# Reordering the seven quarter products of an output projection, and moving two early steps

## The chip, the cores and the metric

The kernel runs on one core of one Trainium2 chip. The metric is the device time of one execution in microseconds (us), as the median of several runs. The engines are TensorE (PE, with its weight loads shown apart as PEld), VectorE (DVE), ScalarE (ACT), GpSimd (POOL) and SyncE (SP), which starts most of the transfers.

## The reference, cut to what matters

Attention with a top-32 mask feeds a SwiGLU feed-forward network. Everything is float32.

```python
batch, n_heads, seq, head_dim = (8, 8, 576, 64)
n_tokens, d_model, d_ff = (4608, 512, 1536)

def _attn_ref(q, k, v):
    scores = scale * np.matmul(q, k.transpose(0, 1, 3, 2))
    kth = np.partition(scores, -top_k, axis=-1)[..., -top_k:-top_k + 1]   # top_k = 32
    scores = np.where(scores >= kth, scores, -1e9)
    scores = scores - np.max(scores, axis=-1, keepdims=True)
    attn = np.exp(scores)
    attn = attn / (np.sum(attn, axis=-1, keepdims=True) + 1e-09)
    return np.matmul(attn, v)

def _moe_ref(x, w_gate, w_val, w_out):      # x: attention output, (4608, 512)
    g = x @ w_gate
    silu = g * (1.0 / (1.0 + np.exp(-g)))
    return (silu * (x @ w_val)) @ w_out
```

## The kernel before: the parts that matter here

The attention works in 160 *units*: one batch, one tile of queries (128 rows, or the last 64), one pair of heads. Each unit passes through a pipeline that spans several turns: scores on TensorE, the top-32 search on VectorE (`select`), the mask added on GpSimd (`penalize`), the exponential on ScalarE (`weigh`), the scaling (`normalize`), a transposition on TensorE (`turn`) and the product with V (`values`). Beside it runs the feed-forward network in 18 *blocks* of 256 tokens. It is a Python generator (`feed`) that is advanced in *pieces* within each turn. A piece is either half of a product or half of a quarter product, and a credit decides how many pieces a turn holds.

Every engine executes its instructions in the order in which this program issues them. So the place at which a piece stands in a turn decides what an engine has to finish before it may go on.

One turn, cut to its order:

```python
        # turn n, head
        next(nxt, None)                  # odd n: scores of units n+1, n+2 (TensorE, ScalarE copies)
        next(nxt, None)
        if 0 <= n - 1 < NU:
            penalize(n - 1)              # GpSimd: bias (L391), e += sc (L393)
        flush(on_pool)                   # queued GpSimd work
        flush(on_act)                    # queued ScalarE work
        if n % 2 == 1 and n >= 5:
            finish_units([n - 5, n - 4]) # values
        early[0]()
        run(nxt)
        if 0 <= n - 1 < NU:
            weigh(n - 1)                 # ScalarE: exp (L402)
        dve(2, beside=False)
        # ...
        pieces(2)
        flush(on_act)
        if 0 <= n - TURN < NU:
            run(turn(n - TURN))          # transposes (L431), copies et (L432)
        dve(1)
        dve(1)
        next(norm, None)
        run(norm)                        # ScalarE: e *= 1/tot (L417)
        next(ahead, None)
        pieces(1)
        run(ahead)
        dve(1)
        pieces(1)
        dve(2)
        run(topk)                        # VectorE: rest of the top-32 search, mask (L381)
        pieces(6)
```

The second matrix product of a block (`silu * val @ w_out`) is done from the second block on with seven products of quarter size instead of eight, and with sums on GpSimd that prepare their operands and collect their results. `first` and `late` are the two halves of the 256 tokens. `T[1]` to `T[7]` are prepared combinations of `w_out`, `hs[0]` to `hs[5]` are the six tiles of the activation, and `s32` reuses the memory of the block's input `x`. Line numbers are those of the profile.

```python
        DH = DM // 2
        y_ps = ps_f.tile([P, 2, DH], FP32, tag="f", name="y_ps")   # tag "f": 3 buffers
        x_ps = ps_f.tile([P, 2, DH], FP32, tag="f", name="x_ps")
        def quarter(i, ps):
            for m in range(MQ):                        # MQ = 6
                s, r = m // 2, m % 2
                lhsT = {
                    1: lambda: hs[s][:, r, first],
                    2: lambda: hs[s + MS // 2][:, r, first],
                    3: lambda: hs[s][:, r, late],
                    4: lambda: hs[s + MS // 2][:, r, late],
                    5: lambda: hs[s][:, r, late],
                    6: lambda: s32[:, m],
                    7: lambda: s32[:, m],
                }[i]()
                nc.tensor.matmul(ps, lhsT, T[i][m], start=m == 0, stop=m == MQ - 1)  # L606
                if m % 3 == 2:
                    yield 0.75
        for s in range(MS // 2):                       # first sum, L613
            nc.gpsimd.tensor_tensor(s32[:, 2*s:2*s+2], hs[s][:, :, first], hs[s][:, :, late], ALU.subtract)
        yield from quarter(1, y_ps[:, 0])
        flush(on_act)
        flush(on_pool)
        for s in range(MS // 2):                       # second sum, L621
            nc.gpsimd.tensor_tensor(hs[s][:, :, late], hs[s][:, :, late], hs[s + MS // 2][:, :, late], ALU.add)
        yield from quarter(7, x_ps[:, 1])
        for s in range(MS // 2):                       # third sum, L626
            nc.gpsimd.tensor_tensor(s32[:, 2*s:2*s+2], hs[s][:, :, late], hs[s][:, :, first], ALU.subtract)
        yield from quarter(5, x_ps[:, 0])
        # keep_x: ScalarE copies x_ps to a (L633), GpSimd o = a0 + a1 (L592)
        on_act.append(keep_x)
        # keep_y: ScalarE copies y_ps to b (L640), GpSimd sum_up: three sums (L592)
        yield from quarter(6, y_ps[:, 1])
        on_act.append(keep_y)
        flush(on_act)
        flush(on_pool)
        for s in range(MS // 2):                       # fourth sum, L654
            nc.gpsimd.tensor_tensor(hs[s][:, :, late], hs[s + MS // 2][:, :, first], s32[:, 2*s:2*s+2], ALU.subtract)
        y_ps2 = ps_f.tile([P, DH], FP32, tag="f", name="y_ps")
        yield from quarter(2, y_ps2[:])
        # rest_y: ScalarE copies y_ps2 to o (L664), GpSimd o += b0 (L592)
        on_act.append(rest_y)
        x_ps2 = ps_f.tile([P, 2, DH], FP32, tag="f", name="x_ps")
        yield from quarter(4, x_ps2[:, 1])
        yield from quarter(3, x_ps2[:, 0])
        # rest_x: ScalarE copies x_ps2 (L676), GpSimd adds a (L592), stores
```

Before the first turn the loads and the first scores are issued. `rounding` and `early` advance the preparation of the weights: a transfer, two ScalarE steps (L121, L123), a GpSimd step (L126), VectorE and GpSimd steps (L130, L133), and a last VectorE step (L136). The VectorE steps are issued between those of the top-32 search.

```python
    load_all(0)
    rounding(2)
    load_all(1)
    run(fetch(0))          # transposes of the first pair's K and Q
    run(scores([0]))
    run(fetch(1))          # those of the second pair
```

Of the kernel before, what the change touches and what calls it, by code (L numbers as in the profile page):

```python
# [10 lines left out]
ALU = mybir.AluOpType  # L11
FP32 = mybir.dt.float32
# [4 lines left out]
P = 128  # L17
# [11 lines left out]
def kernel(  # L29
# [41 lines left out]
    nc = tc.nc  # L71
# [8 lines left out]
    MS = MC // 2  # L80
# [13 lines left out]
    ps_f = ctx.enter_context(tc.tile_pool(name="ps_f", bufs=3, space=PSUM))  # L94
# [117 lines left out]
    early = [lambda: None]  # L212
# [67 lines left out]
    def prep(i):  # L280

        parts = raw.pop(i)
        slab = slabs.tile([P, JP + S], FP32, tag="kqT", name="kqT")
        ahead = NHP <= i and i + 1 < len(pairs)
        for what, at in ((0, 0), (2, JP), (1, S)):
            ps = ps_t.tile([P, 512], FP32, tag="t", name="kqps")
            if what == 2:
                nc.tensor.transpose(
                    ps[:, 0:P], parts[2].rearrange("p h d -> p (h d)"), ident[:]
                )  # L290
                for d in HALVES:
                    nc.scalar.copy(klast[pairs[i][1]][d, d], ps[d, 0:R])
                nc.scalar.copy(slab[:, at : at + R], ps[:, R:P])
                if ahead:
                    load(i + 1, 2)
                yield
                continue
            for c in range(J):
                nc.tensor.transpose(
                    ps[:, c * P : (c + 1) * P],  # L300
                    parts[what][:, c].rearrange("p h d -> p (h d)"),
                    ident[:],
                )
            nc.scalar.copy(slab[:, at : at + JP], ps[:])

            if ahead and what == 0:
                load(i + 1, 1)
            elif ahead and i + 2 < len(pairs):
                load(i + 2, 0)
        preps[i] = slab  # L310
# [8 lines left out]
    def scores(ns):  # L319

        def bank(name):
            return ps_t.tile([P, 512], FP32, tag="t", name=name)

        qt = units[ns[0]][1]
        wide = R if qt == J else P
        at = JP if qt == J else S + qt * P
        queries = slice(at, at + wide)
        of = [(preps[units[n][0] * NHP + units[n][2]], units[n][2]) for n in ns]
        first = [bank("s")] if qt == J else [bank("s") for _ in HALVES]
        last = bank("last")  # L330
        for u, (slab, hp) in enumerate(of):
            if qt < J:
                nc.tensor.matmul(  # L333
                    last[:, u * P : (u + 1) * P], slab[:, queries], klast[hp][:]
                )
            else:
                for d in HALVES:
                    nc.tensor.matmul(
                        last[d, u * P : u * P + R], slab[d, queries], klast[hp][d, d]
                    )  # L340
        for u, (slab, hp) in enumerate(of):
            if u == 0:
                mains = first
            elif qt == J:
                mains = [bank("s")]
            else:
                mains = [bank("s") for _ in HALVES]
            for hh, d in enumerate(HALVES):
                ps = mains[0][d, :] if qt == J else mains[hh][:]
                nc.tensor.matmul(ps, slab[d, queries], slab[d, 0:JP])  # L350
            yield
            sc = work.tile([P, 2 * S], FP32, tag="sc", name="sc", bufs=3)
            state[ns[u]] = dict(sc=sc)
            nc.scalar.copy(sc[:, JP : JP + wide], last[:, u * P : u * P + wide])  # L354
            for hh, ps in enumerate(mains):
                nc.scalar.copy(sc[:, hh * (S + R) : hh * (S + R) + JP], ps[:])  # L356
# [137 lines left out]
    on_act, on_pool = [], []  # L494

    def flush(queue):
        while queue:
            queue.pop(0)()
# [7 lines left out]
    def feed(kb):  # L506
# [5 lines left out]
        hs = []  # L512

        def product(w, s, then):
# [17 lines left out]
        first, late = slice(0, P), slice(P, BLK)  # L532

        s32 = x[:].rearrange("p a b -> p (a b)")[:, 0 : MQ * P].rearrange(
            "p (m t) -> p m t", t=P
        )
# [20 lines left out]
        o = ffn.tile([P, 2, DM], FP32, tag="o", name="o", bufs=1)  # L557
# [27 lines left out]
        while len(T[3]) < MQ:  # L585
            next(weight)
        DH = DM // 2
        y_ps = ps_f.tile([P, 2, DH], FP32, tag="f", name="y_ps")
        x_ps = ps_f.tile([P, 2, DH], FP32, tag="f", name="x_ps")

        def tt(out, in0, in1):
            nc.gpsimd.tensor_tensor(out, in0, in1, ALU.add)  # L592

        def quarter(i, ps):
            for m in range(MQ):
# [10 lines that stand above are left out]
                nc.tensor.matmul(  # L606
                    ps, lhsT, T[i][m], start=m == 0, stop=m == MQ - 1
                )
                if m % 3 == 2:
                    yield 0.75  # L610

        for s in range(MS // 2):
            nc.gpsimd.tensor_tensor(  # L613
                s32[:, 2 * s : 2 * s + 2], hs[s][:, :, first], hs[s][:, :, late], ALU.subtract
            )
        yield from quarter(1, y_ps[:, 0])
        flush(on_act)
        flush(on_pool)

        for s in range(MS // 2):  # L620
            nc.gpsimd.tensor_tensor(  # L621
# [7 lines left out]
        yield from quarter(5, x_ps[:, 0])  # L629
        a = ffn.tile([P, 2, DH], FP32, tag="gv", name="p57", bufs=3)  # L630

        def keep_x():
            nc.scalar.copy(a[:], x_ps[:])  # L633
            on_pool.append(lambda: tt(o[:, 1, DH:], a[:, 0], a[:, 1]))

        on_act.append(keep_x)
        b = ffn.tile([P, 2, DH], FP32, tag="gv", name="p16", bufs=3)

        def keep_y():
            nc.scalar.copy(b[:], y_ps[:])  # L640

            def sum_up():
                tt(b[:, 1], b[:, 0], b[:, 1])
                tt(o[:, 1, DH:], o[:, 1, DH:], b[:, 1])
                tt(a[:], a[:], b[:, 1:2].to_broadcast([P, 2, DH]))

            on_pool.append(sum_up)

# [4 lines that stand above are left out]
        for s in range(MS // 2):  # L653
# [3 lines left out]
                s32[:, 2 * s : 2 * s + 2],  # L657
                ALU.subtract,
            )
        y_ps2 = ps_f.tile([P, DH], FP32, tag="f", name="y_ps")  # L660
        yield from quarter(2, y_ps2[:])

        def rest_y():
            nc.scalar.copy(o[:, 0, 0:DH], y_ps2[:])  # L664
            on_pool.append(lambda: tt(o[:, 0, 0:DH], o[:, 0, 0:DH], b[:, 0]))

        on_act.append(rest_y)
        x_ps2 = ps_f.tile([P, 2, DH], FP32, tag="f", name="x_ps")
        yield from quarter(4, x_ps2[:, 1])
        yield from quarter(3, x_ps2[:, 0])  # L670
# [20 lines left out]
    def piece():  # L691

        if len(on_act) > 1:
            flush(on_act)
        while True:
            if not current:
                if not todo or done.get(todo[0], 0) < NHP * BLK:
                    return 0
                flush(on_act)
                flush(on_pool)  # L700
                current.append(feed(todo.pop(0)))
            cost = next(current[0], 0)
            if cost == 0:
                current.pop()
                continue
            return cost

    def fetch(n):

        b, qt, hp = units[n]  # L710
        i = b * NHP + hp
        if qt == 0:
            yield from prep(i)
# [20 lines left out]
    def run(steps):  # L734
        for _ in steps:
            pass
# [10 lines left out]
    load_all(1)  # L747
    run(fetch(0))
    run(scores([0]))
    run(fetch(1))  # L750
    credit = [0.0]
    no = iter(())
# [119 lines left out]
```

## Time and profile before

| | before |
|---|---|
| time, median of 3 runs (lowest to highest) | 1862.27 us (1861.88 to 1864.19) |
| span of the profiled execution | 1858.6 us |
| PE busy | 1713.0 us, 92% |
| DVE busy | 1641.1 us, 88% |
| ACT busy | 1197.0 us, 64% |
| POOL busy | 1015.3 us, 55% |
| mean granted clock of TensorE | 0.955 of full speed |

Busy shares are means over the whole span. From about 20 to 200 us VectorE is busy nearly all the time and TensorE about half of it; from about 260 us TensorE is busy nearly all the time, and the last 100 us belong to TensorE with the last blocks. A line of the timeline gives start, length, engine, line, operation, tiles and count, and in brackets the idle time of the engine before it and what ended that.

### The profile page before, as it was taken

To read this page: it belongs to the slowest core of one execution; us is meant where nothing else is said; L and a number is where in the kernel's file an instruction comes from. 1 tells how busy PE (TensorE), PEld (TensorE's weight loads), DVE (VectorE), ACT (ScalarE), POOL (GpSimd) and SP (SyncE) were. 2 spreads that over 40 slices of the span, in tenths; PEclk is the share of its full clock that TensorE was granted. 3 is DMA by queue.
4 is the path that set the end of the run, shared out by engine and by line. 5 is a ranking of instruction groups with operands and counts; after the bars stand their busy time and mean duration, and the time that the engine had idled before them with its cause. 6 is when DMAs were issued, how large, how long until landed. Compare 5 with 4: busy or idle time off the path is not lost.

```text
span 1858.6 us, 29975 instructions
## 1 busy us (share of the span) xinstructions
PE 1713.0 (92%) x10500; PEld 1394.9 (75%) x10500; DVE 1641.1 (88%) x3409; ACT 1197.0 (64%) x2879; POOL 1015.3 (55%) x932
## 2 busy tenths in 40 slices
PE   4467889989999999999999999999999999999998
PEld 2236658768888878787888877878888878787886
DVE  6999999999999989998999979998999979999300
ACT  4656766667666676576767675766776667575431
POOL 3555747636565546555465636565457544656444
PEclk8558999989999999999999999999999999999999
DMA  6332220001200020001200021000300011000000
GB/s 174 91 91 85 63 63 27 1 12 30 57 4 12 1 64 26 12 1 27 50 25 1 13 52 38 1 12 7 71 14 12 1 45 26 12 1 12 1 12 12
DMA packets 104534, 58.56 MB, mean 32 GB/s; under 512 B 83904, under 2 KB 92096, under 8 KB 104384
## 3 DMA queue, kind: packets, MB, share of 16 engines
q1 hardware_dynamic: 103328, 56.39, 11.5%
q8 instruction: 83, 1.36, 0.3%
q14 instruction: 67, 0.55, 0.1%
q10 hardware_dynamic: 1056, 0.26, 0.1%
HBM read 47.19 MB, written 9.44 MB: 30 GB/s over the span
## 4 chain that ended last, share of the span: by engine, by line
PE 68%; ACT 10%; POOL 6%; DVE 2%; issue 1%; POOLq 0%; ACTq 0%
PE f L520 37%; PE av L459 7%; PE s L350 7%; PE x_ps L606 5%; PE etps L431 5%; PE y_ps L606 3%; ACT e L402 3%; POOL e L393 2%; ACT et L432 2%; PE av L466 2%; ACT e L417 2%; POOL p L592 1%; ACT sc L356 1%; PE last L333 1%; POOL h L654 1%; DVE m L371 1%
## 5 line engine op out<-in xcount | busy, mean ns | idle before, releaser
L371 DVE MAX8 m<-e 128x8 f32<-128x576 f32 x864 | 612.7, 744 | 2.2
L393 POOL TENSOR_TENSOR e<-e,sc 128x1152 f32<-128x1152 f32 (+1 forms) x160 | 382.8, 2392 | 336.8 <-DVE e L381 282.1
L375 DVE MATCH_REPLACE8 e<-m,e 128x576 f32<-128x576 f32 x576 | 423.0, 740 | 0.0
L520 PE MATMUL f<-xT,wv 128*128 128x256 f32 x1728 | 396.7, 380 | 0.0
L520 PE MATMUL f<-xT,wg 128*128 128x256 f32 x1728 | 395.5, 380 | 0.0
L520 PEld LDWEIGHTS f<-xT,wg 128*128 128x128 f32 x1728 | 323.9, 190 | 42.2 <-issue 0.5
L520 PEld LDWEIGHTS f<-xT,wv 128*128 128x128 f32 x1728 | 322.9, 190 | 41.1 <-ACT half_g L546 0.2
L402 ACT ACTIVATE e<-e,bias 128x576 f32<-128x576 f32 x288 | 224.5, 793 | 96.3 <-POOL e L393 96.3
L371 DVE MAX8 m<-sc 128x8 f32<-128x576 f32 x288 | 204.8, 746 | 63.8 <-ACT sc L356 45.2
L350 PE MATMUL s<-kqT 64*128 64x512 f32 (+1 forms) x640 | 197.5, 665 | 50.8 <-ACT et L432 41.1
L431 PE MATMUL etps<-ident,e 128*128 128x128 f32 x1312 | 178.9, 281 | 45.2 <-ACT e L417 21.8
L417 ACT ACTIVATE e<-e,tot 128x576 f32<-128x576 f32 x288 | 212.9, 794 | 5.6 <-DVE tot L414 5.6
L375 DVE MATCH_REPLACE8 e<-m,sc 128x576 f32<-128x576 f32 x288 | 211.4, 739 | 0.0
L431 PEld LDWEIGHTS etps<-ident,e 128*128 128x128 f32 x1312 | 157.4, 145 | 67.8 <-issue 32.8
L459 PEld LDWEIGHTS av<-et,v 128*64 128x64 f32 x2560 | 141.9, 147 | 79.2 <-ACT sc L356 66.8
L432 ACT COPY et<-etps 128x512 f32<-128x512 f32 (+1 forms) x448 | 182.3, 480 | 17.1 <-PE etps L431 17.1
L381 DVE TENSOR_SCALAR e<-sc,m 128x576 f32<-128x576 f32 x288 | 189.3, 693 | 1.1
L548 POOL TENSOR_TENSOR h<-h,half_g 128x512 f32<-128x512 f32 x108 | 139.3, 1290 | 91.4 <-ACT h L547 88.5
L356 ACT COPY sc<-s 128x512 f32<-128x512 f32 x288 | 159.5, 610 | 42.2 <-PE s L350 42.2
L553 POOL TENSOR_TENSOR h<-h,val 128x512 f32<-128x512 f32 x108 | 139.0, 1287 | 86.1 <-ACT val L552 83.1
L459 PE MATMUL av<-et,v 128*64 128x128 f32 (+1 forms) x2560 | 162.6, 282 | 12.1 <-ACT sc L356 11.3
L354 ACT COPY sc<-last 128x128 f32<-128x128 f32 (+1 forms) x160 | 42.5, 266 | 185.0 <-PE last L333 157.8
(75 smaller groups left out, 2043.4 us busy)
## 6 DMA issues: line engine op xcount, KB each, us to landing
v<-in_v_dram SPq DMA_DIRECT2D x32, 256.0 KB, 2.9
kq_in<-in_k_dram SPq DMA_DIRECT2D x63, 128.0 KB, 2.8
kq_in<-in_q_dram SPq DMA_DIRECT2D x63, 128.0 KB, 2.7
w<-in_moe_w_gate_dram SPq DMA_DIRECT2D x12, 512.0 KB, 3.8
w<-in_moe_w_val_dram SPq DMA_DIRECT2D x12, 512.0 KB, 3.7
w<-in_moe_w_out_dram SPq DMA_DIRECT2D x12, 512.0 KB, 3.4
out_dram<-o SPq DMA_DIRECT2D x40, 128.0 KB, 2.4
out_dram<-o SPq DMA_DIRECT2D x16, 256.0 KB, 2.4
```

The costliest lines, as they stand in the source:

```text
L350: nc.tensor.matmul(ps, slab[d, queries], slab[d, 0:JP])
L356: nc.scalar.copy(sc[:, hh * (S + R) : hh * (S + R) + JP], ps[:])
L371: nc.vector.max(m[:, t, 8 * r : 8 * r + 8], cur[:, hs])
L375: nc.vector.match_replace(e[:, hs], m[:, t, 8 * r : 8 * r + 8], cur[:, hs], LOWEST)
L381: nc.vector.tensor_scalar(e[:, hs], sc[:, hs], m[:, t, TOP_K - 1 : TOP_K], FAR, ALU.is_lt, ALU.mult)
L393: nc.gpsimd.tensor_tensor(e[:, every], e[:, every], sc[:, every], ALU.add)
L402: nc.scalar.activation(e[:, hs], e[:, hs], AF.Exp, bias=bias[:, t : t + 1], scale=scale, accum_out=tot[:, t : t + 1],)
L417: nc.scalar.mul(e[:, hs], e[:, hs], tot[:, t : t + 1])
L431: nc.tensor.transpose(ps[:, c * P : (c + 1) * P], e[:, k0 : k0 + P], ident[:])
L432: nc.scalar.copy(et[:, c0 : c0 + cn, :], ps[:, 0 : cn * P].rearrange("p (c j) -> p c j", c=cn),)
L459: nc.tensor.matmul(av[d, 0:ql], v_c, moving, start=c == 0, stop=last and c == J)
L520: nc.tensor.matmul(ps[:, i, :], w[:, kc, m * P : (m + 1) * P], x[:, kc, :], start=(kc == 0), stop=(kc == KC - 1),)
```

## The change

The quarter products run in the order 1, 2, 7, 5, 6, 4, 3 instead of 1, 7, 5, 6, 2, 4, 3. Product 2 needs no sum, so it stands ahead of product 7, which needs the first sum. The first sum is no longer issued where the generator stands but is put into the queue of GpSimd work, which is emptied at a turn's head (after `penalize`) or after product 1. The copy of product 2's result is issued at once behind it, and the sum that adds `b0` to it moves into `sum_up`, ahead of the fourth sum. Last, `early` is called once more before the second pair's K and Q are transposed, so that ScalarE does the first two rounding steps of the first weight piece there. No work is added or removed: the arithmetic and the counts of instructions stay.

```diff
+        y_ps2 = ps_f.tile([P, DH], FP32, tag="f", name="y_ps")
         y_ps = ps_f.tile([P, 2, DH], FP32, tag="f", name="y_ps")
-        x_ps = ps_f.tile([P, 2, DH], FP32, tag="f", name="x_ps")
 ...
-        for s in range(MS // 2):
-            nc.gpsimd.tensor_tensor(
-                s32[:, 2 * s : 2 * s + 2], hs[s][:, :, first], hs[s][:, :, late], ALU.subtract
-            )
+        def third():
+            for s in range(MS // 2):
+                nc.gpsimd.tensor_tensor(
+                    s32[:, 2 * s : 2 * s + 2],
+                    hs[s][:, :, first],
+                    hs[s][:, :, late],
+                    ALU.subtract,
+                )
+
+        on_pool.append(third)
         yield from quarter(1, y_ps[:, 0])
         flush(on_act)
         flush(on_pool)
+        yield from quarter(2, y_ps2[:])
+        on_act.append(lambda: nc.scalar.copy(o[:, 0, 0:DH], y_ps2[:]))
+        flush(on_act)
+        x_ps = ps_f.tile([P, 2, DH], FP32, tag="f", name="x_ps")
 ...
                 tt(a[:], a[:], b[:, 1:2].to_broadcast([P, 2, DH]))
+                tt(o[:, 0, 0:DH], o[:, 0, 0:DH], b[:, 0])
 ...
-        y_ps2 = ps_f.tile([P, DH], FP32, tag="f", name="y_ps")
-        yield from quarter(2, y_ps2[:])
-
-        def rest_y():
-            nc.scalar.copy(o[:, 0, 0:DH], y_ps2[:])
-            on_pool.append(lambda: tt(o[:, 0, 0:DH], o[:, 0, 0:DH], b[:, 0]))
-
-        on_act.append(rest_y)
         x_ps2 = ps_f.tile([P, 2, DH], FP32, tag="f", name="x_ps")
         yield from quarter(4, x_ps2[:, 1])
         yield from quarter(3, x_ps2[:, 0])
 ...
     run(scores([0]))
+    early[0]()
     run(fetch(1))
```

## The prediction

> **What bounds the kernel now.** I read the busy times first, then the same by stages, then the waits, and last the timeline around single blocks. The page's first part says what to look at:
>
> ```profile
> PE 1713.0 (92%) x10500; PEld 1394.9 (75%) x10500; DVE 1641.1 (88%) x3409; ACT 1197.0 (64%) x2879; POOL 1015.3 (55%) x932
> ```
>
> By stages (busy time in windows): DVE 97.7 of 100 us and PE 67.2 from 100 to 200 us; DVE 50.0 of 50 and PE 41.0 from 340 to 390; then PE 96 to 100 of every 100 us up to 1750. So VectorE sets the pace up to about 385 us, TensorE from there. The waits name what could be won:
>
> ```profile
> ACT e L402 <- POOL e L393: 96.3, 24, 8.1
> POOL xT L613 <- PE f L520: 57.2, 14, 10.5
> DVE size L130 <- POOL size L126: 10.2, 6, 5.9
> PEld x_ps L606 <- POOL h L654: 6.3, 6, 2.1
> ```
>
> The columns are total us, times, longest. The first sum (L613) blocks GpSimd for 57 us, as it overwrites the block's input and has to wait for the products that read it. TensorE hardly ever waits for the sums themselves (6.3 us). In the block whose first quarter starts at 732 us the timeline of GpSimd and then TensorE shows what does reach TensorE:
>
> ```profile
> 750.80 0.73 POOL L592 TENSOR_TENSOR p<-p 128x256 f32<-128x256 f32 x1 [2.22 <-ACT p L640]
> 753.53 2.52 POOL L654 TENSOR_TENSOR h<-h,xT 128x256 f32<-128x256 f32 x3
> 756.20 2.62 POOL L393 TENSOR_TENSOR e<-e,sc 128x1152 f32<-128x1152 f32 x1
> 758.97 2.62 POOL L393 TENSOR_TENSOR e<-e,sc 128x1152 f32<-128x1152 f32 x1
> ...
> 761.61 3.78 PE L350 MATMUL s<-kqT 64*128 64x512 f32 x6 [2.54 <-ACT et L432]
> 765.32 3.46 PE L459 MATMUL av<-et,v 128*64 128x128 f32 x32
> ```
>
> Two masks (L393) stand back to back behind the collecting sums and the fourth sum. ScalarE, waiting 8.13 us for the first mask, holds up the copies that free TensorE's banks: 2.54 us idle, and 3.46 us instead of the usual 1.97 for the V products. In other blocks nothing is lost; that at 545 us:
>
> ```profile
> 561.16 2.75 PE L606 MATMUL y_ps<-wo,h 128*128 128x256 f32 x12
> 563.75 1.15 PE L431 MATMUL etps<-ident,e 128*128 128x128 f32 x9
> 564.73 2.76 PE L606 MATMUL x_ps<-t,h 128*128 128x256 f32 x12
> 567.60 2.86 PE L606 MATMUL x_ps<-wo,h 128*128 128x256 f32 x12
> ```
>
> Products 2, 4 and 3 follow with less than 0.3 us between. The fourth sum, on which product 3 depends, starts at 566.83: it just makes it because product 2 lies between. The start of the kernel:
>
> ```profile
> 11.49 1.42 DVE L371 MAX8 m<-sc 128x8 f32<-128x576 f32 x2 [9.52 <-ACT sc L356]
> 18.84 0.43 DVE L130 TENSOR_SCALAR size<-size 128x512 int32<-128x512 int32 x1 [5.93 <-POOL size L126]
> 17.42 0.69 ACT L121 ACTIVATE size<-w 128x512 f32<-128x512 f32 x1
> ```
>
> VectorE stands 5.93 us, because ScalarE takes the first weight piece only after the second unit's scores.
>
> **The Trainium skill.** PSUM — Partial Sum Buffer, section Engine vs sequencer instructions, says that the queues of ScalarE, VectorE and GpSimd are strict first-in-first-out and that matmuls start in program order. The trace agrees: ScalarE's exponential waits 8.13 us at 758.86 for the mask while finished transposes lie behind it. GPSIMD Engine Reference, section 3.1 Elementwise — side-by-side cycle accounting, gives about 2.6 cycles per element for a two-input sum; its 1.2 GHz makes 256 elements an estimated 0.55 us plus dispatch. The trace has 0.73 to 0.78 us, which I use. SBUF — State Buffer, section Who interferes with whom, says that VectorE and GpSimd can block each other at a shared port pair; the mask step L381 takes 0.93 us for two at 823.47 and 2.68 at 834.03, beside GpSimd sums. I count nothing for it, as the sums stay. TensorE: Matmul & The Clock Gate, section What's actually happening, says that the granted clock follows recent activity; the stages have 0.53 from 50 to 100 us and 1.00 later. That limits how surely a gain at the start survives.
>
> **The change, part by part.** Nothing is added; what moves is order.
>
> *Start.* ScalarE's steps L121 and L123 can run at 11.9 to 13.1, right behind the copies that end at 11.94; the transfer, issued at 3.66, takes 4.4 us at the median. GpSimd's L126 (0.61) then lets L130 start near 13.3 instead of 18.84: 5.6 us. The second unit's copies slip by 1.2 us, unimportant as VectorE wants them only at about 26. But the second weight piece keeps its ScalarE time near 18.6 and now makes VectorE wait about 0.9 us, the third some 0.4. Gain 4.3 us, carried on as VectorE sets the pace there.
>
> *Piece by piece.* Costs of pieces are unchanged, so turns are cut at the same places. Products 7, 5, 6 come 2.59 us (one quarter) later, and product 6's flush, which issues both copies, the collecting sums and the fourth sum, moves from the 9th to the 11th piece of 14. From the end of `keep_y`'s copy to the first third of the fourth sum it takes 0.73 + 0.73 + 1.27 + 0.73 (the moved sum) + 0.75, about 4.3 us with gaps. Product 4 (2.59) and at most a transposition (0.98) now hide it. What happens depends on where the turn ends.
>
> Blocks at 732, 1205, 1581 (turn ends between pieces 9 and 10) and 826, 1674 (between 10 and 11): the 11th piece now lies in the next turn, behind its `penalize`. In the block at 732 the first mask can start after the third sum, near 746.2, instead of 756.20. Product 6 ends at 751.25, `keep_y`'s copy near 752.9, the fourth sum's first third near 756.5; product 3, ready at 754.8, stalls 1.7 us. But the 2.54 us of idle time and the slow V products go: these end near 763.5 instead of 768.7. Gain 5.2. The same in 1205 (idle 2.53 + 0.65) makes 2.65, in 1581 3.5. In 826 the stall is 2.3 against 2.79 of idle time, gain 0.4; in 1674 with its slow V products (3.58) gain 1.9. Sum: 13.7 us gained.
>
> Blocks at 545, 1016, 1393 (turn ends between 8 and 9): the 11th piece now stands behind the turn's transposes and scalings on ScalarE. Product 6 ends at 563.75, the scalings at 566.96, the copy near 567.5, the first third of the fourth sum near 571.9. Product 3 is ready at 567.3: it stalls 4.6 us against 0.3 before. Loss 4.3 each, 12.9.
>
> Blocks at 631, 1480 (a turn starts at piece 8, its transposition behind 9): the same with scalings to 652.2, the fourth sum at 657.4, product 3 ready at 653.5. Loss 3.8 each, 7.6; the mask behind it slips as much.
>
> Blocks at 932, 1122: product 3 already stalled (1.30 and 1.71 us) and starts 0.8 and 0.95 later. Loss 1.75. Block at 333: product 3 stalls 4.7 us, but VectorE sets the pace and TensorE idles about 9 us after it anyway; a later mask (363.4 for 356.4) costs some: 4. Blocks at 446, 1295: the turn's head hides the sums, 0.5 each. Block at 1758: fourth sum at 1778.7 for product 3 at 1777.6 before, 1.1. Last block: the 1.57 us wait before product 5 goes, product 3 stalls 2.2: 0. Sum of losses 12.9 + 7.6 + 1.75 + 4 + 1 + 1.1 = 28.4.
>
> Net: -4.3 - 13.7 + 28.4 = +10.4 us, 1862.3 + 10.4 = 1872.7; I say 1872.
>
> **The rivals.** (1) The stalls of product 3 are hidden, because TensorE runs behind and other work fills them. Against it: TensorE is in order, and product 3 stands directly behind 4 in eight blocks; for it: two blocks had time to spare. Then only gains remain: about 1845 to 1850. (2) The earlier masks free more than I count: 96 us of ScalarE's waiting hang on them, and 55.8 us of VectorE's waits for `tot`. Yet TensorE's own waits from 330 to 1760 us come to about 38 us, so at most another 10: near 1862. (3) The late fourth sum delays the next mask in every block, and VectorE, 92 to 98% busy, loses those microseconds too: +10 more, near 1883. (4) The gain at the start is lost, as the clock steps of TensorE before 260 us stay at their times: +4.
>
> **Range and chances.** Five of the nine kinds of block have the same sign by simple order (product 3 directly behind a late sum), so I lean to slower by half a per cent; rivals 1 and 3 set the ends: 1853 to 1887. Two per cent is 37 us, beyond either: faster 0.02, same 0.92, slower 0.06.
>
> **What would show it.** Right: the first L130 near 13.3 us and its 5.93 us wait gone; TensorE waiting for L654 about 40 us in all instead of 10; in the blocks of the 732 kind the idle time at the scores gone and the two masks apart; GpSimd's wait at L613 far below 57 us. Wrong: product 3 following 4 without a gap in the 545 kind, or ScalarE's copy L640 ahead of the scalings there. Then the time falls below 1855.

## The result, and the profile after

The changed kernel takes 1877.48 us (median of 4 runs, 1873.33 to 1877.93) against 1862.08 us (1859.9 to 1864.19) of the kernel before, measured beside it. The ratio is 1.0078, with a 95% interval from 1.0059 to 1.0096: slower by 0.8%, some 15 us. The profiled executions have spans of 1875.6 and 1858.6 us.

The busy times, in the first part of the page after, say nothing about it:

```profile
PE 1713.5 (91%) x10500; PEld 1396.4 (74%) x10500; DVE 1624.0 (87%) x3409; ACT 1199.1 (64%) x2879; POOL 1014.1 (54%) x932
```

TensorE has the same busy time as before (1713.0) and the same count, so in sum the 17 us by which the span grew are idle time of TensorE. The waits of the kernel after name them (total us, times, longest):

```profile
ACT e L402 <- POOL e L393: 56.2, 21, 8.4
...
PEld x_ps L606 <- POOL h L666: 47.8, 16, 4.7
PE x_ps L606 <- POOL h L666: 42.0, 15, 4.4
...
POOL xT L614 <- PE f L520: 4.7, 4, 4.0
```

TensorE now waits 42.0 us for the fourth sum (L666, which was L654) and its weight loads 47.8, mostly over the same stretches; before, these were 3.5 and 6.3. The line of before for the 3.5:

```profile
PE x_ps L606 <- POOL h L654: 3.5, 3, 1.7
```

The two longest waits that the prediction listed did shrink: GpSimd's for the block's input from 57.2 to 4.7 us (L613, now L614), and ScalarE's for the masks from 96.3 to 56.2. The kernel is slower all the same. In the block of 545 us the timeline after shows the new wait, on TensorE, then on ScalarE, then on GpSimd:

```profile
559.12 2.76 PE L606 MATMUL x_ps<-t,h 128*128 128x256 f32 x12
566.08 5.33 PE L606 MATMUL x_ps<-wo,h 128*128 128x256 f32 x12 [4.20 <-POOL h L666]
571.25 3.62 PE L520 MATMUL f<-xT,wg 128*128 128x256 f32 x16
...
559.89 1.46 ACT L417 ACTIVATE e<-e,tot 128x576 f32<-128x576 f32 x2
561.24 0.59 ACT L651 COPY p<-y_ps 128x512 f32<-128x512 f32 x1
...
561.90 0.73 POOL L592 TENSOR_TENSOR p<-p 128x256 f32<-128x256 f32 x1 [2.83 <-ACT p L651]
...
564.62 0.72 POOL L592 TENSOR_TENSOR o<-o,p 128x256 f32<-128x256 f32 x1
565.30 2.09 POOL L666 TENSOR_TENSOR h<-h,xT 128x256 f32<-128x256 f32 x3
```

Product 4 ends at 561.88. The copy of `keep_y` (L651) comes behind the two scalings, the four sums that it releases come next (the moved one at 564.62), and then the fourth sum. Product 3 starts 4.20 us late. The second thing to see is its length: 5.33 us for the same twelve matmuls that took 2.86 before. Of the two stretches below, cut around product 3, the first is of after, the second of before (columns: length; busy time of PE, PEld, DVE, ACT, POOL with counts; granted clock; share and GB/s of the transfers):

```profile
566.00:571.30 5.30, 5.22 (x13) 4.21 (x14) 2.53 (x5) 0.00 (x0) 1.39 (x3) 0.52 0.00 0
```

```profile
567.60:570.30 2.70, 2.70 (x13) 2.39 (x13) 2.70 (x7) 0.00 (x0) 2.01 (x3) 1.00 0.00 0
```

The granted clock of TensorE is 0.52 after the wait and 1.00 where there was none. The wait costs twice: once while TensorE stands, once while it runs at half speed behind it.

The displacement of each block is read at the heads of turns, as the difference between the starts of the first score matmuls of the two profiled executions (plus is later):

| blocks | predicted, us | after, us |
|---|---|---|
| start | -4.3 | -3.1 |
| 732, 826, 1205, 1581, 1674 | -13.7 | -11.6 |
| 545, 1016, 1393 | +12.9 | +18.8 |
| 631, 1480 | +7.6 | +8.0 |
| 932, 1122 | +1.75 | +5.1 |
| 333 | +4 | -2.5 |
| 446, 1295 | +1 | 0 |
| last two | +1.1 | +2.3 |
| sum | +10.4 | +17.0 |

### The profile page after: what moved, and what is told of

Read it like the earlier page. It is cut to its first block, busy times and chain, and to the rows that moved or that the text cites. A ratio compares the mean times of both kernels' runs of the same rounds, so it can differ in the third digit from the quotient of the medians.

```text
span 1875.6 us, 29950 instructions
## 1 busy us (share of the span) xinstructions
PE 1713.5 (91%) x10500; PEld 1396.4 (74%) x10500; DVE 1624.0 (87%) x3409; ACT 1199.1 (64%) x2879; POOL 1014.1 (54%) x932
## 4 chain that ended last, share of the span: by engine, by line
PE 77%; ACT 9%; POOL 4%; issue 0%; DVE 0%; DMA 0%; POOLq 0%; ACTq 0%
PE f L520 39%; PE av L459 8%; PE s L350 7%; PE x_ps L606 7%; PE y_ps L606 6%; PE etps L431 5%; ACT e L402 2%; PE av L466 2%; ACT e L417 2%; POOL p L592 2%; ACT et L432 2%; PE last L333 1%; POOL o L592 1%; ACT sc L356 1%; PE o_ps L566 1%; PE kqps L299 1%
## 5 line engine op out<-in xcount | busy, mean ns | idle before, releaser
L402 ACT ACTIVATE e<-e,bias 128x576 f32<-128x576 f32 x288 | 224.5, 794 | 56.2 <-POOL e L393 56.2
L350 PE MATMUL s<-kqT 64*128 64x512 f32 (+1 forms) x640 | 188.4, 656 | 31.0 <-ACT et L432 25.6
L459 PEld LDWEIGHTS av<-et,v 128*64 128x64 f32 x2560 | 135.8, 142 | 76.9 <-ACT sc L356 68.6
L381 DVE TENSOR_SCALAR e<-sc,m 128x576 f32<-128x576 f32 x288 | 171.3, 631 | 1.1
L459 PE MATMUL av<-et,v 128*64 128x128 f32 (+1 forms) x2560 | 156.3, 275 | 11.9 <-ACT sc L356 11.0
```

The lines of the kernel that those rows point to most:

```text
L402: nc.scalar.activation(e[:, hs], e[:, hs], AF.Exp, bias=bias[:, t : t + 1], scale=scale, accum_out=tot[:, t : t + 1],)
L459: nc.tensor.matmul(av[d, 0:ql], v_c, moving, start=c == 0, stop=last and c == J)
```

## The experiments

The theory at the outset: product 3 waits because the fourth sum is issued behind the collecting sums, and these behind a copy on ScalarE; the lost time is that wait plus the half clock behind it. Rival A: the order of the products is itself at fault, since product 2 no longer fills the time. Rival B: the late sums delay the masks, and VectorE loses the time. Rival C: the first sum, queued or not, matters.

**Each part alone.** First the early call added to the kernel before, then the kernel after without it.

```diff
     run(scores([0]))
+    early[0]()
     run(fetch(1))
```

> The kernel before, with nothing but the early rounding steps ahead of the second pair's K and Q. My theory (the start gains, the new order loses): VectorE's first wait of 5.93 us goes, the whole program moves forward by about 3.1 us as in the changed kernel's trace before the first reordered block, so about 1859 us and every later distance between heads of turns as before. Rival (the start's gain is swallowed before the end, by the clock or by TensorE): 1862 us, as before.

It took 1857.57 us, ratio 0.9988 (0.9979 to 0.9996). The profiled execution was the slowest of twelve (1861.98 us). It shows -2.95 us at the start, and no block but those at 1205 and 1581 moves by as much as 1 us. These two carry +2.2 and +1.4: their gaps of 2.5 us were there before, but in this execution a clock of 0.50 follows both (before: 1.00 and 0.66).

> The changed kernel without the early rounding steps: order of products and queued first sum alone. My theory: the start's 3 us are lost and all the rest stays, about 1880 to 1882 us, with TensorE waiting some 42 us for the fourth sum. Rival (the two parts of the change disturb each other, and the slowdown needs both): near 1862 us.

1879.48 us, ratio 1.0095 (1.0078 to 1.0111). So the early call gives some 2 us in the kernel before by the ratios, 3 by the medians, and in the kernel after a difference of the same size, which the overlapping intervals do not resolve. The new order of the products, with the sums that moved with it, costs some 18 to 19 us.

**The fourth sum ahead of the collecting sums.** It needs the third sum, and product 5 to have read the half that it overwrites, and nothing from ScalarE. In the kernel after, its loop is moved up by three lines:

```diff
         yield from quarter(6, y_ps[:, 1])
+        for s in range(MS // 2):
+            nc.gpsimd.tensor_tensor(hs[s][:, :, late], ...)   # fourth sum
         on_act.append(keep_y)
         flush(on_act)
         flush(on_pool)
-        for s in range(MS // 2):
-            nc.gpsimd.tensor_tensor(hs[s][:, :, late], ...)
```

> The changed kernel with one thing moved: the fourth sum is issued on GpSimd ahead of the collecting sums (and of the two copies they wait for) instead of behind them. It needs only product 5 and the third sum, which are done. My theory (product 3 waits for the fourth sum, because only product 4 lies between): TensorE's wait for the fourth sum falls from 42 us to under 5, the gains of the other blocks stay, and the time falls to between 1826 us (the sum of the gains by block in the changed kernel's trace) and 1845 us (if VectorE then sets the pace). Rival (the queued first sum and the later third sum, at which GpSimd waits 38 us, are what costs): the time stays above 1865 us.

1824.26 us, ratio 0.9801 (0.9786 to 0.9816): 53 us faster than the changed kernel, and 2% faster than the one before. The timeline of the same block in this kernel, TensorE and then GpSimd:

```profile
556.50 2.75 PE L606 MATMUL x_ps<-t,h 128*128 128x256 f32 x12
559.09 2.75 PE L606 MATMUL x_ps<-wo,h 128*128 128x256 f32 x12
...
553.14 2.38 POOL L663 TENSOR_TENSOR h<-h,xT 128x256 f32<-128x256 f32 x3
...
559.28 0.73 POOL L592 TENSOR_TENSOR p<-p 128x256 f32<-128x256 f32 x1 [2.84 <-ACT p L651]
```

The fourth sum (now L663) runs at 553.14, in time in which GpSimd otherwise stands waiting for the copy, and product 3 follows product 4 at once. TensorE's wait for the fourth sum is no longer in the list. GpSimd still waits 2.84 us for the copy, but with nothing behind it that TensorE needs. The first part of the page also shows what the clock had cost:

```profile
PE 1695.2 (93%) x10500; PEld 1387.3 (76%) x10500; DVE 1624.0 (89%) x3409; ACT 1199.1 (66%) x2879; POOL 1013.2 (56%) x932
```

The same 10500 matmuls keep TensorE busy 18.3 us less than in the kernel after (1713.5). Of these, 2.9 us fall to the first 1263 matmuls, ahead of the first reordered product (234.8 us busy, 237.7 in after). Of the 53 us between the two profiles some 15 are thus faster matmuls behind that point, and nearly all the rest is waiting that is gone.

**The same in the old order.** If the order of the products is at fault (rival A), the move should help little where product 2 lies between. The run also has the early call.

> The old order 1, 7, 5, 6, 2, 4, 3 with the fourth sum ahead of the collecting sums and the early rounding steps. My theory (the gain of the third experiment comes from the masks that the new order lets past the collecting sums, and the fourth sum's place only removes the price): the masks stay stuck, only the stalls of the blocks at 932 and 1122 go, 1852 to 1858 us. Rival (the fourth sum's place is the whole gain, whatever the order): 1830 us or less.

1830.04 us, ratio 0.9822 (0.9808 to 0.9837), far below what I had expected. The place of the fourth sum cost the kernel before some 30 us too (the early call's share taken off), only elsewhere: product 3 hardly waited for it (3.5 us in all), but in blocks like that at 732 us it stood ahead of the masks. In the block at 732 us GpSimd now runs so, in the old order with the sum (L651) ahead:

```profile
737.09 1.60 POOL L651 TENSOR_TENSOR h<-h,xT 128x256 f32<-128x256 f32 x2 [1.24 <-PE x_ps L606]
740.41 0.73 POOL L592 TENSOR_TENSOR o<-p 128x256 f32<-128x256 f32 x1 [1.73 <-ACT p L633]
743.37 0.73 POOL L592 TENSOR_TENSOR p<-p 128x256 f32<-128x256 f32 x1 [2.23 <-ACT p L640]
...
746.49 2.88 POOL L393 TENSOR_TENSOR e<-e,sc 128x1152 f32<-128x1152 f32 x1
```

and TensorE at the scores behind it:

```profile
752.16 1.98 PE L350 MATMUL s<-kqT 64*128 64x512 f32 x6 [0.53 <-ACT et L432]
754.79 1.97 PE L459 MATMUL av<-et,v 128*64 128x128 f32 x32 [0.65 <-ACT sc L356]
```

From the first collecting sum that waits for `keep_y`'s copy to the mask there are now 3.1 us (743.37 to 746.49); before there were 5.4 (750.80 to 756.20), the 2.52 us of the fourth sum among them. The idle time at the scores falls from 2.54 to 0.53 us, and the scores and the V products take 1.98 and 1.97 us, not 3.78 and 3.46.

**The moved `b0` sum alone.** The kernel after, with the sum that adds `b0` to product 2 taken out of `sum_up` and queued behind the fourth sum:

```diff
                 tt(a[:], a[:], b[:, 1:2].to_broadcast([P, 2, DH]))
-                tt(o[:, 0, 0:DH], o[:, 0, 0:DH], b[:, 0])
 ...
         # behind the loop of the fourth sum
+        on_pool.append(lambda: tt(o[:, 0, 0:DH], o[:, 0, 0:DH], b[:, 0]))
```

> The changed kernel with the sum that adds b0 put back behind the fourth sum. My theory: each of the some 15 stalls of product 3 gets 0.7 us shorter, 10 us in all, a little more where the shorter stall keeps the clock up: 1864 to 1868 us. If the moved sum were the whole cause of the slowdown: 1850 us or less. If GpSimd's place did not matter: 1877 us.

1859.51 us, ratio 0.999 (0.9983 to 0.9997): 18 us below the kernel after (0.9% by the ratios), more than expected. TensorE's wait for the fourth sum falls by 10.2 us only:

```profile
PE x_ps L606 <- POOL h L665: 31.8, 15, 3.8
```

That is 15 waits, each shorter by 0.7 us, the length of the sum. The busy time of TensorE falls by another 5.9 us (1707.6 against 1713.5). In the block at 932 us the wait goes from 2.29 to 1.60 us, and the first six matmuls of product 3 from 2.53 us to 1.56: the shorter wait no longer drops the clock, in the execution profiled. One sum of 0.7 us per block, ahead of a late one, thus costs 0.9% of the kernel, which is the whole slowdown: with it out of the way the new order does as well (0.999) as the old one with the early call alone (0.9988). The expectation put such a case at 1850 us or less. That is not reached, as the stalls that are left, 31.8 us of waiting, use up what other blocks gain (5.3 us in that at 732).

**Filling the wait with useless work.** To part the clock from the waiting: the kernel after, with product 4 done a second time between 4 and 3, into the half bank that product 3 overwrites right after. Its result is discarded, and it adds 17 times 2.6, or 44 us of matmuls.

```diff
         yield from quarter(4, x_ps2[:, 1])
+        for m in range(MQ):
+            nc.tensor.matmul(
+                x_ps2[:, 0], hs[m // 2 + MS // 2][:, m % 2, late], T[4][m],
+                start=m == 0, stop=m == MQ - 1,
+            )
         yield from quarter(3, x_ps2[:, 0])
```

> The changed kernel with useless work added: product 4 once more between 4 and 3, into the half of the bank that product 3 then overwrites; 17 blocks by 2.6 us of TensorE time. My theory (a stall of product 3 costs twice: the wait, and then the half clock that the idle time brings, 5.3 us instead of 2.7 for its matmuls): in the blocks of the 545 kind the repeat fills the wait, product 3 runs at full clock, and the loss by block falls from 6.6 to about 4.3 us although work is added; over the whole program the saved clock and the repeats in blocks without a stall about cancel, 1868 to 1880 us. Rival (product 3 is slow because its thirds arrive one by one from GpSimd, not because of the clock): the loss in those blocks stays at 6.5 us or grows, and the time goes above 1885 us.

1872.38 us, ratio 1.0048 (1.0032 to 1.0065): with 44 us more work, 5 us below the kernel after by the medians, where the intervals just touch. The timeline of this kernel in the block of 545 us, with the repeat at L675, and the stretch around product 3:

```profile
564.55 2.75 PE L675 MATMUL x_ps<-t,h 128*128 128x256 f32 x12
568.93 2.86 PE L606 MATMUL x_ps<-wo,h 128*128 128x256 f32 x12 [1.62 <-POOL h L666]
```

```profile
568.90:571.60 2.70, 2.67 (x12) 2.39 (x13) 2.47 (x5) 0.00 (x0) 1.34 (x2) 1.00 0.02 6
```

The same late fourth sum now meets a TensorE that has been busy: 1.62 us of waiting, and the clock stays at 1.00. The sum still comes in three parts, so it was not their coming one by one that made product 3 slow. The three blocks of this kind are 4.1, 4.1 and 4.1 us later than before instead of 6.6, 5.5 and 6.7. What is left is the repeat (2.6) and the shorter wait (1.6), so these blocks lose nothing to VectorE or the masks, and rival B falls there. In the blocks at 446 and 1295 us, where there was no wait to fill, the repeat costs its full 2.6 us.

**The first sum issued directly.** The kernel after, with the first sum issued where the generator stands, not queued; then the same with the fourth sum ahead.

```diff
-        on_pool.append(third)
+        third()
```

> The changed kernel with the first sum issued where the generator stands, as before, instead of queued. My theory (the place of the first sum does not reach TensorE): GpSimd waits some 50 us at it again, and the time stays within 3 us of the changed kernel's, 1874 to 1880 us. Rival (queueing it is what brings the masks forward in the blocks of the 732 kind): their gains of 2 to 3 us a block vanish, 1888 us or more.

1878.92 us, ratio 1.0083 (1.0068 to 1.0098). GpSimd waits 57.6 us for the block's input again, and the time stays:

```profile
POOL xT L614 <- PE f L520: 57.6, 15, 10.5
```

> The kernel of the third experiment (new order, fourth sum ahead) with the first sum issued directly instead of queued. My theory: within 3 us of the third experiment's 1824 us. Rival (the queue matters once the stalls are gone): 1832 us or more.

1824.94 us, ratio 0.9799 (0.9785 to 0.9814), the same as with the queue (0.9801). Rival C falls: nobody waited behind GpSimd there.

**The masks ahead of the collecting sums too.** What is left of the difference between the orders (1824.9 us in the run just above and 1830.0 in the old order, measured together; the intervals just overlap) could be the mask, which in the old order stands behind the collecting sums. Leaving out the second flush lets these sums wait in the queue until the next turn's `penalize` has been issued. First on the new order, then on the old one, each with the fourth sum ahead and the early call:

```diff
         on_act.append(keep_y)
         flush(on_act)
-        flush(on_pool)
```

> The kernel of the third experiment (new order, fourth sum ahead) with the collecting sums left in the queue after product 6, so that the next turn's mask goes ahead of them on GpSimd. My theory (a mask stuck behind the collecting sums, which wait for ScalarE's copies, holds up ScalarE and then TensorE): the 1.66 us of idle time in the blocks at 631 and 1480 go, and the time falls from 1824 to between 1816 and 1822 us. Rival (the collecting sums' place costs nothing any more): 1824 us, or more where the late sums hold up the next block's buffers.

1819.86 us, ratio 0.9778 (0.9765 to 0.9792), against 0.9801 with the flush; the intervals overlap. The gaps of TensorE at which the expectation aimed are gone. In the block at 631 us, first with the flush, then without:

```profile
652.58 0.66 PE L299 MATMUL kqps<-ident,kq_in 128*128 128x128 f32 x4 [1.66 <-ACT et L432]
...
651.86 0.60 PE L299 MATMUL kqps<-ident,kq_in 128*128 128x128 f32 x4
```

> The same in the old order 1, 7, 5, 6, 2, 4, 3 (fourth sum ahead, collecting sums left in the queue, early rounding steps). My theory (what the new order has over the old, once the fourth sum is ahead, is only that it lets masks past the collecting sums): it comes within 3 us of the kernel with the new order, 1816 to 1824 us. Rival (the order of the products is worth something by itself): it stays at the seventh experiment's 1830 us.

1820.30 us, ratio 0.9782 (0.9768 to 0.9795). GpSimd in the block at 732 us, old order:

```profile
736.99 1.60 POOL L651 TENSOR_TENSOR h<-h,xT 128x256 f32<-128x256 f32 x2 [1.24 <-PE x_ps L606]
...
738.72 2.65 POOL L393 TENSOR_TENSOR e<-e,sc 128x1152 f32<-128x1152 f32 x1
741.33 0.73 POOL L592 TENSOR_TENSOR o<-p 128x256 f32<-128x256 f32 x1
743.27 0.73 POOL L592 TENSOR_TENSOR p<-p 128x256 f32<-128x256 f32 x1 [1.21 <-ACT p L640]
```

The mask goes 7.8 us earlier than in the same order with the flush (738.72 against 746.49), and the idle time at the scores is gone. The two orders now agree within 0.5 us. So once the sums are issued in the right order, the order of the products, which is what the change is about, is worth nothing that these runs can see (rival A). Either version is 2.2% faster than the kernel before.

## Why the prediction was right and wrong

The time, 1877 us, is inside the predicted range and above the 1872 us named. Its main mechanism held, and it gave the right direction. That the sum over the blocks came within 7 us is partly luck: it was too low by 5.9 us in the 545 kind, 3.4 at 932 and 1122 and 2.1 in the 732 kind, and too high by 6.5 at 333.

- *The wait.* "TensorE waiting for L654 about 40 us in all": 42.0. (The "10" set beside it was the waits of matmuls and of weight loads added, 3.5 and 6.3; that of the matmuls was 3.5.) "ScalarE's copy L640 ahead of the scalings" was named as the sign of an error; the copy came behind them. In the 545 kind the stall was to be 4.6 us and was 4.20. That the late fourth sum is what the change costs is shown by the run with that sum ahead. That the sum moved in front of it decides between a loss and none is shown by the run with the `b0` sum behind.
- *The term that was mis-sized.* "Loss 4.3 each" was the stall less 0.3, and was 6.6, 5.5 and 6.7 us. The sum left out that TensorE runs at about half speed behind a stall (5.33 us for product 3 instead of 2.86). The filled wait shows that this, and not a later loss on VectorE, is the missing part. Of the 6.6 us by which the sum of all blocks was too low, this kind has 5.9. The blocks at 932 and 1122 us have 3.4 for the same reason: the stall at 932 grew by about the predicted amount (1.30 to 2.29 us, predicted 0.8), but crossed into the range in which the clock falls.
- *A right size with a wrong cause.* In the 732 kind "ScalarE ... holds up the copies that free TensorE's banks: ... 3.46 us instead of the usual 1.97 for the V products". The idle time was read rightly. The slow V products were not held up; they ran at half clock, as the window of the kernel before shows:

```profile
764.50:768.00 3.50, 3.50 (x28) 2.69 (x28) 3.50 (x7) 0.66 (x2) 2.19 (x3) 0.50 0.16 59
```

 TensorE is busy through all of it, at a granted clock of 0.50. Taking the 2.54 us gap away restored the speed (the fourth sum ahead in the old order), so that the time was there to be won, whatever its cause: -11.6 us for -13.7. After the change the two masks of this block start at 750.62 and 762.85, apart as predicted, but product 3 waits 2.05 us and then takes 4.54, which gives part of it back.
- *The blocks at 631 and 1480 us*: +8.0 for +7.6. Here the half clock did not come in one of the two (the wait was 2.94 us in both), so that the agreement is partly chance.
- *The block at 333 us* has the wrong sign, -2.5 for +4. Product 3 does stall there, 4.45 us for the predicted 4.7, but nothing follows from it as VectorE sets the pace. The prediction added a cost for the later mask that did not appear. Which step gained the 2.5 us wasn't tested.
- *The start*: -3.1 for -4.3. The first L130 of the kernel after:

```profile
12.77 0.43 DVE L130 TENSOR_SCALAR size<-size 128x512 int32<-128x512 int32 x1 [0.35 <-POOL size L126]
```

 It starts even before the predicted 13.3 us. The later pieces cost more than counted: the third, put at 0.4 us, makes VectorE wait 1.35.
- *The rivals.* (1), stalls hidden behind other work, is refuted by the 42.0 us. (3), VectorE losing the time as well, is about as far above the result (1883) as the named time is below it, and the filled wait leaves it no room in the 545 kind. (4) is refuted by the early call alone, which keeps most of the gain at the start. (2), the masks, gave nothing beyond the estimate in the change itself. The runs with the masks first show that there was something to win: by the ratios 0.4% in the old order (0.9822 to 0.9782), and perhaps 0.2% in the new (0.9801 to 0.9778, where the intervals overlap).

What the prediction did not ask is why the fourth sum had to stand behind the collecting sums at all. It is a matter of three lines, it hampered both kernels, and it decides the matter. How much of each block's loss is wait and how much is clock is measured only where useless work fills the wait, and in the busy time as a whole; which gaps of about 2 to 3 us drop the clock differs between executions (see the end), so that single blocks are uncertain by some 2 us.

## What to carry to other kernels

On an engine that works in order, issue what already has its inputs ahead of what still waits for another engine: three sums moved in front of such a wait brought 53 us in the changed kernel, while the order of the products brought nothing that could be seen. Count a gap of TensorE of more than 2 us as the gap and, where the clock falls, up to 1.7 or 3.4 us more for the slower matmuls behind it (the last section has the windows). Before removing a long wait of an engine off the critical path, look for someone who waits behind it: GpSimd's 57 us had nobody.

## What was not expected of the hardware

A gap of TensorE is followed by half speed sooner than I had thought. TensorE: Matmul & The Clock Gate of the Trainium skill, section What's actually happening, says that the clock has two states and falls after at least one idle window of about 3.4 us, and that the window is free-running. In nine profiles (before, after and the first seven runs), I took each gap of at least 1 us after 400 us and the mean granted clock of the 3.4 us behind it:

| gap | half clock behind it (0.50 to 0.69) |
|---|---|
| 3.5 us and more | 12 of 12 |
| 2.0 to 2.95 us | 22 of 36 |
| 1.1 to 1.9 us | 5 of 53 |

The two states agree with the page: the clock records of all twelve profiles hold 0.50 and 1.00 alone. So does the free-running window: in each profile every change of the clock lies on one grid with steps of 3.41 us. The idle time that suffices does not agree: gaps of 2.05 to 2.95 us, well under 3.4, dropped the clock in more than half of the cases, and the measurement decides.

The grid also tells which gaps do. Of all windows between two lines of it that lie between 400 and 1790 us and ran at full clock, in the twelve profiles, I took TensorE's idle time in the window and the clock of the next:

| idle in the window | half clock in the next |
|---|---|
| 2.0 us and more | 31 of 31 |
| 1.0 to 1.96 us | 5 of 68 |
| less | 0 of 4737 |

So the same gap drops the clock or not by where it falls. The 2.94 us at 658 us in after were cut by a line of the grid into 1.82 and 1.12 us, and the clock stayed at 1.00; the 2.27 us there with the `b0` sum behind lay in one window, and 0.52 followed. The half clock lasted one window or two each time (3.41 or 6.83 us); half of that, 1.7 or 3.4 us, is the most that it can have cost. The five short gaps of the first table are all of 1.41 us and lie at the end of the kernel, among other gaps.
